# Where the last tile's second layer is cut: column 320 in place of column 256

## The chip, the cores and the metric

The kernel runs on one core of one Trainium2 chip. The metric is the time of one execution in device microseconds; for the kernel before it is the median of three runs.

## The reference

Attention over a sliding window with a few fixed positions at the start, then a layer norm and a two-layer network with a residual. `q`, `k`, `v` are float32 of 4 batches, 8 heads, 768 positions, 64 numbers each.

```python
keep = (key position < 4) | (0 <= query position - key position < 128)
a    = softmax(q @ k.T / sqrt(64), over the keys that are kept)
x    = heads of (a @ v) side by side                   # 4 x 768 x 512
xn   = (x - mean(x)) / sqrt(var(x) + 1e-6) * g_ln
out  = x + relu(xn @ w_ch1) @ w_ch2                    # w_ch1 512 x 2048, w_ch2 2048 x 512
```

The output is float32, 4 x 768 x 512.

## The kernel before

The 3072 rows are 24 tiles of 128 rows; two tiles make a chunk, so there are 12 chunks. Attention runs per tile, the network per chunk.

**How the order is made.** Nothing is issued as it is written down. Each step is an operation with a list of engines that may do it, a planned duration on each, a priority and the buffers that it reads and writes. A planner (`Plan.run`) places the operations by planned time, picks engine and buffer, and then every engine's instructions are emitted in that order. The planned durations are numbers in the program: a matmul group of the second layer counts 0.865 us for 512 columns and in proportion for fewer (line 1078), and the eviction's duration also grows with its width (line 1082).

**The network of a chunk** (`mlp`, from line 1028). The first layer makes eight buffers `h` of 128 x 512 bf16 from the normalised rows, 64 matmuls of 256 columns in all but the first chunk (line 1046), each followed by a relu on ScalarE or VectorE (lines 1056 and 1058). The second layer goes tile by tile. For each tile 16 matmuls, one for each block of 128 of the 2048 hidden values, are summed up in one PSUM bank (line 1074). The weight that is loaded is a 128 x 128 block of `h`, the data that is streamed past it are columns of `w2`. An operation holds four such matmuls.

**The last tile.** For tiles 0 to 22 the second layer is one piece of 512 columns. The last tile, number 23, is divided into pieces by columns: `LAST_CUTS` (line 228) gives the cuts, and the loop of line 1067 runs over the pieces. Each piece has a PSUM buffer of its own, 16 matmuls of its own width, one eviction on VectorE (line 1083: PSUM times the row's factor plus `x`, into `ot` in float32) and one store to `out` (line 1087). So every block of `h` is loaded as a weight once for each piece. The first piece's store is issued by ScalarE's queue, because `len(cuts) - f` is 3 there, which is in `LAST_ACT`; the second piece's is issued by SP.

**What stands at the end.** A check of the softmax sums has been made by then: VectorE counts bad values (line 1114), a small matmul sums them up (line 1119), and a flag is written (line 1121). Every engine reads the flag (line 1159) and branches on it (line 1161); the rare path behind the branch is a slow general kernel that isn't taken here. A tiny matmul (line 1125, "hold") reads the last column of the last tile's `ot` and so makes TensorE wait for the last eviction. SP's last store is kept back until all the rest has been emitted, behind SP's own read of the flag (line 1160), and after its branch SP waits for all outstanding semaphores (in the profile at line 1196).

Of the kernel before, what the change touches and what calls it, by code (L numbers as in the profile page):

```python
# [224 lines left out]
SW_Q = (0.25, 0.7, 0.9)  # L225

LOW, HIGH = 1e-9, 1e9
LAST_CUTS, LAST_ACT = (0, 256, 512), (3,)
NEG = -1e30
NEVER = -1e9  # L230
BIG = 3.3e38
# [969 lines left out]
```

## Time and profile before

| | |
|---|---|
| median of three runs | 216.78 us (216.47, 216.78, 216.9) |
| the profiled execution | 217.02 us |
| its span, first to last instruction | 215.5 us |
| granted TensorE clock over the span | 1.000 |
| TensorE busy | 205.9 us, 96% |
| VectorE, ScalarE, GpSimd busy | 115.3, 110.0, 111.8 us |
| matmuls of the second layer (line 1074) | 84.5 us busy |
| matmuls of the first layer (line 1046) | 79.3 us busy |

PE is TensorE's matmul row and PEld its weight loads, which run beside it. DVE is VectorE, ACT ScalarE, POOL GpSimd, SP SyncE; a q behind a name (SPq) is that engine's queue, with its DMA issues and waits. A line such as `L1074 PE MATMUL one<-w,h` names the line of the kernel, the engine, the instruction, and what is written from what, without buffer numbers. A single matmul's duration in a row is longer than the step from one to the next, because matmuls overlap; what counts in a stream is the step. Some records of matmuls can be missing from a trace.

### The profile page before, as it was taken

What the parts mean: (1) busy time and instruction counts of PE and PEld (TensorE: products, weight loads), DVE (VectorE), ACT (ScalarE), POOL (GpSimd) and SP (SyncE); (2) the same over time, 40 slices, a digit from 0 to 9 for tenths busy, and PEclk for the clock granted to TensorE, in tenths of its full rate; (3) what the DMA queues carried; (4) which work ended last, traced back from release to release, by engine and by line L of the source; (5) the groups of instructions that cost most, each with busy time, mean ns of one, the idle gap of its engine ahead of it and who ended that gap; (6) DMA issues with size and microseconds to landing.
All of it is one profiled execution on the core that took longest, in us unless ns stands there. A gap on an engine that the chain in (4) does not pass through costs nothing.

```text
span 215.5 us, 6660 instructions
## 1 busy us (share of the span) xinstructions
PE 205.9 (96%) x2743; PEld 144.1 (67%) x2765; DVE 115.3 (53%) x315; ACT 110.0 (51%) x178; POOL 111.8 (52%) x166
## 2 busy tenths in 40 slices
PE   7798899999999999999999999999999999999994
PEld 2467875765865875864865865864865865865853
DVE  5589875698445446446345446446355345444011
ACT  3796387496562562562562562562562562530610
POOL 7978632499972881871971981871971211201000
PEclk9999999999999999999999999999999999999999
DMA  5999999999999999799799899899799302202103
GB/s 156 187 190 205 193 206 192 167 180 132 154 187 169 123 125 145 87 175 151 123 115 170 112 147 145 111 122 168 111 141 149 80 3 76 73 0 76 49 2 105
DMA packets 104554, 28.04 MB, mean 130 GB/s; under 512 B 94788, under 2 KB 101576, under 8 KB 104520
## 3 DMA queue, kind: packets, MB, share of 16 engines
q0 software_dynamic: 69872, 13.18, 90.2%
q1 hardware_dynamic: 33448, 13.74, 35.7%
q10 hardware_dynamic: 1200, 0.66, 1.1%
q8 instruction: 22, 0.36, 0.7%
q14 instruction: 12, 0.10, 0.2%
HBM read 27.43 MB, written 6.29 MB: 156 GB/s over the span
## 4 chain that ended last, share of the span: by engine, by line
PE 88%; DVE 5%; DMA 3%; issue 2%; ACT 1%; ACTq 0%; DVEq 0%
PE one L1074 39%; PE one L1046 36%; PE pair L980 3%; DMA natf<-in_q_dram 3%; PE one L953 2%; PE one L960 2%; PE one L969 1%; DVE st L881 1%; DVE xnt L909 1%; PE one L988 1%; PE one L1039 1%; DVE x L873 1%; DVE xc L885 1%; PE pair L605 1%; PE pair L730 1%
## 5 line engine op out<-in xcount | busy, mean ns | idle before, releaser
L1074 PE MATMUL one<-w,h 128*128 128x512 bf16 (+1 forms) x378 | 84.5, 371 | 2.2 <-issue 1.6
L1056 ACT ACTIVATE h<-one 128x512 bf16<-128x512 f32 x93 | 55.6, 598 | 47.3 <-PE one L1046 42.6
L1046 PE MATMUL one<-xnt,w 128*128 128x256 bf16 x704 | 79.3, 273 | 0.0
L1046 PEld LDWEIGHTS <-w 128*128 128x128 bf16 x704 | 68.6, 98 | 10.4
L1074 PEld LDWEIGHTS <-h 128*128 128x128 bf16 x400 | 37.3, 98 | 39.6
L998 ACT ACTIVATE pe<-pair 128x768 bf16<-128x768 f32 x36 | 27.2, 809 | 41.0 <-PE pair L980 41.0
L645 POOL DMA_DIRECT2D vn<-in_v_dram x59 | 38.7, 695 | 10.9 <-DMA w<-in_moe_w_ch_dram 6.8
L890 POOL TENSOR_SCALAR st<-st 128x1 f32<-128x1 f32 x24 | 8.9, 369 | 62.4 <-DVE st L883 61.9
L1021 DVE RECIPROCAL rec<-one 128x4 f32<-128x4 f32 x36 | 6.4, 178 | 62.5 <-PE one L969 51.1
L1083 DVE SCALAR_TENSOR_TENSOR ot<-one,st,x 128x512 f32<-128x512 f32 (+1 forms) x25 | 18.2, 727 | 13.9 <-PE one L1074 9.0
L891 POOL TENSOR_TENSOR st<-st,mhalf 128x1 f32<-128x1 f32 x24 | 17.0, 707 | 2.0
L881 DVE BATCH_NORM_STATS2 st<-x 128x6 f32<-128x512 bf16 x24 | 16.7, 695 | 0.8
L1023 DVE TENSOR_TENSOR x<-one,rec 128x256 bf16<-128x256 f32 x36 | 15.3, 425 | 1.2
L703 POOL DMA_DIRECT2D nat<-in_k_dram x16 | 14.9, 932 | 1.9 <-DMA natp<-in_q_dram 1.6
L703 POOL DMA_DIRECT2D nat<-in_q_dram x16 | 14.3, 905 | 0.0
L1003 DVE TENSOR_TENSOR pe<-pe,band 128x768 bf16<-128x768 bf16 x24 | 12.2, 552 | 0.0
L885 DVE TENSOR_SCALAR xc<-x,st 128x512 bf16<-128x512 bf16 x24 | 9.3, 387 | 0.9
L980 PE MATMUL pair<-qT,kT 64*64 64x128 bf16 (+1 forms) x528 | 9.2, 204 | 0.0
L953 PEld LDWEIGHTS <-pe 128*128 128x128 bf16 (+1 forms) x144 | 6.2, 97 | 2.9 <-issue 0.8
L778 ACT ACTIVATE pe<-pair 128x1024 bf16<-128x1024 f32 (+1 forms) x8 | 7.1, 916 | 1.8 <-PE pair L730 1.4
L1039 PE MATMUL one<-xnt,w 128*128 128x128 bf16 x128 | 8.0, 220 | 0.0
L980 PEld LDWEIGHTS <-kT 64*64 64x64 bf16 x528 | 7.2, 108 | 0.4 <-ACT w L1110 0.4
(112 smaller groups left out, 165.7 us busy)
## 6 DMA issues: line engine op xcount, KB each, us to landing
out_dram<-ot SPq DMA_DIRECT2D x23, 256.0 KB
w<-in_moe_w_ch_dram POOLq DMA_DIRECT2D x8, 512.0 KB, 14.5
nat<-in_k_dram POOLq DMA_DIRECT2D x16, 128.0 KB, 5.1
nat<-in_q_dram POOLq DMA_DIRECT2D x16, 128.0 KB, 5.6
vn<-in_v_dram POOLq DMA_DIRECT2D x44, 32.0 KB, 6.0
vn<-in_v_dram POOLq DMA_DIRECT2D x15, 64.0 KB, 6.3
natp<-in_k_dram POOLq DMA_DIRECT2D x3, 256.0 KB, 14.3
vn<-in_v_dram POOLq DMA_DIRECT2D x6, 128.0 KB, 9.2
```

Source lines behind the costliest of these rows:

```text
L645: P.op(f"vld{t}_{i}", {"POOL": (0.8, 0.85)}, prio + 0.001 * i, lambda e, p0=p0, n=n, hs=hs, src=src: G.dma_start(m.t[p0:p0 + n, hs, 0:64], ...
L703: lambda e, nat=nat, ap=ap: G.dma_start(nat.t, ap), writes=[nat], dma=SW, after=gate(c))
L881: P.op(f"bn{t}", {"DVE": fix(0.60)}, d + 0.12, lambda e: V.bn_stats(st.t[:, 8:14], x.t), reads=[x], writes=[st, mv])
L891: G.tensor_tensor(st.t[:, 16:17], st.t[:, 17:18], mhalf, op=ALU.pow)),
L980: nc.tensor.matmul(pps[u].t[64 * g:64 * g + 64, h2, col + c0:col + c0 + n], lhsT=kt.t[rs, hp, k0:k0 + 64], rhs=qT.t[rs, hp, q0:q0 + n], st ...
L998: nc.scalar.activation(pes[j].t.rearrange("p a b -> p (a b)")[:, 0:768].rearrange("p (a b) -> p a b", a=2), pps[j].t[:, :, 0:384], AF.Exp, ...
L1003: V.tensor_mul(at_s, at_s, band[j] if r > 1 else edge[r][j].unsqueeze(1).to_broadcast([128, 4, 192]))
L1023: P.op(f"x{t - 1}{u}", {"DVE": dve(256)}, d + 0.051 + 0.002 * u, lambda e, u=u, rc=rc, pv=pv: V.tensor_tensor(x.t[:, 256 * u:256 * u + 256 ...
L1046: nc.tensor.matmul(ph.t[:, 256 * s:256 * s + 256], lhsT=w1[ht // 4][:, j, 128 * (ht % 4):128 * (ht % 4 + 1)], rhs=xnt.t[:, j, :], start=j ...
L1056: nc.scalar.activation(hb.t, ph.t, AF.Relu)
L1074: nc.tensor.matmul(pc.t[:, 0:wd], lhsT=(h1[2 * s + i].t[:, 128 * ii:128 * ii + 128] if by_tile else h1[ht // 2].t[:, 256 * (ht % 2) + 128 ...
L1083: V.scalar_tensor_tensor(ot.t[:, sl], in0=pc.t[:, 0:wd], scalar=st.t[:, 16:17], in1=x.t[:, sl], op0=ALU.mult, op1=ALU.add),
```

## The change

The last tile's first piece takes columns 0 to 319 and its second piece columns 320 to 511, 192 of them, where both had 256. The number of matmuls, weight loads, evictions and stores is as before, and so is the engine of each store. The planned durations of the two pieces change with the widths. No other tile is touched.

```diff
-LAST_CUTS, LAST_ACT = (0, 256, 512), (3,)
+LAST_CUTS, LAST_ACT = (0, 320, 512), (3,)
```

## The prediction

> **What bounds the kernel now.** I read the views in this order: the chain of waits over the whole span, to see which engine sets the end; then the chain, the timeline and the groups from 208 us on, which is where the last tile's second layer runs; then the rows on the last stores, because a change at the very end can only act through what comes behind the last matmul.
>
> The chain of the whole span (its share by engine, and three pieces of its 256, each with start, length and number of instructions):
>
> ```profile
> PE 88%; DVE 5%; DMA 3%; issue 2%; ACT 1%; ACTq 0%; DVEq 0%
> ...
> 25.89 1.79 PE one L1039 x32
> ...
> 39.32 1.73 PE one L1074 x8
> ...
> 54.25 6.99 PE one L1046 x64
> ```
>
> TensorE carries 88% of the chain, so the kernel is one long row of matmuls, and a matmul saved anywhere would be worth its own time. The three pieces give what one matmul costs in a row: 1.79 us / 32 = 55.9 ns at 128 columns, 6.99 / 64 = 109.2 ns at 256, 1.73 / 8 = 216.3 ns at 512. From 128 to 256 that is 53.3 ns for 128 columns, from 256 to 512 107.1 ns for 256: 0.417 ns a column both times, with some 2.5 ns on top for each matmul. All three use a new 128x128 weight for every matmul, as the last tile does.
>
> The end of the chain, from 208.6 us on:
>
> ```profile
> 208.55 3.72 PE one L1074 x33
> 212.28 0.03 issue
> 212.31 0.02 DVEq L1083
> 212.33 0.04 issue
> 212.37 0.50 DVE ot L1083
> 212.87 0.04 issue
> 212.91 0.19 PE one L1125 x2
> ```
>
> The reader sees the last 32 matmuls (16 for columns 0 to 255, 16 for 256 to 511; the 33rd is the last of the tile before), then the last eviction on VectorE, then the small matmul that is tied to it. The chain as printed stops there; the store that follows the same eviction is found in the timeline (start, length, instruction, and in brackets the idle time before it):
>
> ```profile
> 208.86 0.75 DVE L1083 SCALAR_TENSOR_TENSOR ot<-one,st,x 128x512 f32<-128x512 f32 x1 [2.61 <-PE one L1074]
> 209.64 3.58 SPq L1087 DMA_DIRECT2D out_dram<-ot  x2
> 210.72 0.48 DVE L1083 SCALAR_TENSOR_TENSOR ot<-one,st,x 128x256 f32<-128x256 f32 x1 [1.11 <-PE one L1074]
> 211.24 0.38 ACTq L1087 DMA_DIRECT2D out_dram<-ot  x1
> 212.37 0.48 DVE L1083 SCALAR_TENSOR_TENSOR ot<-one,st,x 128x256 f32<-128x256 f32 x1 [1.16 <-PE one L1074]
> ```
>
> The row of SP merges the issue for the tile before and the last issue, and ends at 209.64 + 3.58 = 213.22. One such issue takes 0.33 us (row below), so the last store is issued from 212.88 on, 0.03 us after the eviction ended at 212.85. What is moved, by stretch (length; TensorE, weight loads, VectorE, ScalarE, GpSimd; granted clock, share of the 16 DMA engines, GB/s):
>
> ```profile
> L1087 SPq DMA_DIRECT2D out_dram<-ot x2: 332/334/337, 209.6 to 212.9; - x2
> ...
> 210.40:211.35 0.95, 0.95 (x12) 0.85 (x10) 0.48 (x1) 0.00 (x0) 0.00 (x0) 1.00 0.73 276
> 212.10:212.65 0.55, 0.16 (x2) 0.00 (x0) 0.28 (x1) 0.00 (x0) 0.00 (x0) 1.00 0.70 238
> 212.65:213.60 0.95, 0.19 (x2) 0.09 (x2) 0.20 (x1) 0.00 (x0) 0.00 (x0) 1.00 0.02 9
> 213.60:214.10 0.50, 0.00 (x0) 0.00 (x0) 0.00 (x0) 0.00 (x0) 0.00 (x0) 1.00 0.70 244
> 214.10:214.25 0.15, 0.00 (x0) 0.00 (x0) 0.00 (x0) 0.00 (x0) 0.00 (x0) 1.00 0.50 116
> ```
>
> Three bursts stand apart: the store of the tile before (512 columns) from 210.4, the first piece's from 212.1, the second piece's from 213.6. Each begins about 0.8 us after its issue began (209.64, 211.24, 212.88). Behind the last one SP walks through its closing waits, shown here for the stretches 213.7 to 214.48 and 214.5 to 214.7 (shortest, median and longest in ns, first and last start):
>
> ```profile
> L1196 SPq EVENT_SEMAPHORE  x11: 28/28/28, 213.8 to 214.4; - x11
> ...
> L1196 SPq EVENT_SEMAPHORE  x1: 28/28/28, 214.6 to 214.6; - x1
> ```
>
> Eleven waits start between 213.8 and 214.4, one every 0.06 us, and the twelfth at 214.6, about 0.1 us later than that step would have it. By its place it is the one that the last store's landing holds up. The span ends at 215.5, some 0.9 us of closing work later, and the profiled execution took 217.02 us, 1.5 us more than its span.
>
> **The change, part by part.** Before 208.6 us nothing differs: the same instructions in the same order. The planner places work by time, but in the timeline all that starts after the first matmul of this tile is what is quoted above, so no other work is there to be put elsewhere.
>
> *Matmuls.* Sixteen of 256 columns become sixteen of 320, and sixteen of 256 become sixteen of 192. By 0.417 ns a column, 64 columns are 26.7 ns: 135.9 and 82.5 ns. The first piece ends 16 x 26.7 = 0.43 us later, the second takes 0.43 us less, and the last matmul ends where it did: 16 x (135.9 + 82.5) = 3.49 us against 32 x 109.2 = 3.49. No row has 192 or 320 columns; 192 lies between 128 and 256 and 320 between 256 and 512, and these rows stand on one line, so I take zero. The bounds: a straight line cannot make it better than zero, and the loads (first rival) make it at most 0.43 us worse.
>
> *The first piece's eviction and store.* The groups by shape (number, busy us, mean ns, idle us):
>
> ```profile
> L1083 DVE SCALAR_TENSOR_TENSOR ot<-one,st,x 128x512 f32<-128x512 f32 x23 | 17.2, 748 | 11.7 <-PE one L1074 6.8 <-POOL st L891 4.7
> L1083 DVE SCALAR_TENSOR_TENSOR ot<-one,st,x 128x256 f32<-128x256 f32 x2 | 1.0, 484 | 2.3 <-PE one L1074 2.3
> ```
>
> (748 - 484) / 256 = 1.03 ns a column, so 320 columns take 550 ns and 192 take 418. The first eviction starts 0.43 us later, at 211.15, and ends at 211.70. Behind it on VectorE stands the last eviction, which waited 1.16 us for TensorE before and starts at 212.37; 0.67 us of that cover is left. The store on ScalarE's queue is issued at 211.73 and not at 211.24, and nobody but the closing walk waits for that queue. Its transfer starts at 212.6. A 512-column store keeps the engines 0.73 x 0.95 = 0.694 us, a 256-column one 0.70 x 0.55 = 0.385, so 64 columns are (0.694 - 0.385) / 4 = 0.077 us, and it ends near 213.2. The last store's transfer begins at 213.5, so 0.3 us of the gap that was 212.65 to 213.60 stays open. Cost nothing. If that cover were gone, the two would share the same 16 engines and the end would move by what overlaps, 0.46 us at the worst.
>
> *The last eviction.* It starts at the same time and takes 418 ns and not 484: 0.066 us off the path. SP's last issue and the tied matmul both wait for it and move with it, and so does the walk of waits.
>
> *The last store.* It moves three quarters of the bytes in the same 128 row pieces: 0.077 us off, by the same rows. The lead-in of 0.8 us didn't follow the size (512 and 256 columns above), so I leave it. The bounds: nothing, if SP's walk is what ends last, and 0.077 in full, as the twelfth wait is late by about 0.1 us. I take it in full, since 0.1 is more than 0.077, though only just.
>
> The sum: 0 - 0.066 - 0.077 = -0.143 us. On the profiled execution 217.02 becomes 216.88. That execution was 0.24 above the median of the three runs, 216.78, so the prediction is **216.64 us**, 0.07% less. A difference under about 0.2% (0.43 us, as far as the three runs lie apart) is no more than a measurement of this kernel can tell from no change.
>
> **The rivals.**
>
> *Slower: the weight loads set the pace of the narrow piece.* Every matmul needs a fresh load, and these are the loads of this tile and those of the 128-column matmuls:
>
> ```profile
> L1074 PEld LDWEIGHTS <-h 128*128 128x128 bf16 x31 | 3.0, 98 | 0.5
> L1039 PEld LDWEIGHTS <-w 128*128 128x128 bf16 x128 | 7.2, 98 | 0.1
> ```
>
> A load shows 98 ns, and in this tile the loads fill 3.0 of 3.49 us, with little room. At 192 columns a matmul streams 82.5 ns, less than the load; the point at which it would decide is 98 ns, some 230 columns. If the pace could not fall under 98 ns, the second piece would lose 16 x (98 - 82.5) = 0.25 us; if it stayed at today's 109.2, 0.43. With the 0.143 gained, the time would be 0.10 to 0.28 above the median, up to **217.06**. The Trainium skill (TensorE: Matmul & The Clock Gate, "LDWEIGHTS (loading the stationary operand)") has the load time as columns over 1.2, which for 128 is 107 ns, and by that as the pace the piece would lose an estimated 16 x (107 - 82.5) = 0.39 us; it speaks against the change. Against the rival stands the second row: 128 loads of 98 ns fill only 7.2 us, 56 ns apiece, and the first fence has 32 of those matmuls at 55.9 ns. So loads overlap one another, and a pace well under 82.5 ns was kept with the same weight shape. Chance 0.06.
>
> *Slower: the two last stores collide.* The gap of 0.3 us is eaten if the first store's transfer is late by more than that; the worst is 0.46 - 0.14 = 0.32 above the median, **217.10**. The steady lead-in of 0.8 us speaks against it. Chance 0.02.
>
> *Little gained: SP's walk or the closing work ends last.* Then only the eviction's 0.066, or nothing, comes off: **216.71 to 216.78**. For it speaks that the twelfth wait is late by hardly more than the 0.077 I take off. Chance 0.10.
>
> *Faster by more: the store shrinks as a whole.* From issue (212.88) to the twelfth wait (214.6) are 1.7 us; a quarter of that is 0.43, and with the eviction **216.28**, 0.23% less. Against it: the lead-in was alike for 512 and 256 columns, and the walk's own step allows only about 0.1 beyond the eviction. Chance 0.04.
>
> *The cut does something else,* since the planner also uses the widths for its times and could order or place the end differently. With one eviction and one store per piece and nothing else left to run, there is nothing to exchange: **216.78**. Chance 0.02.
>
> **How the numbers follow.** The forecast has 0.76. The runs of before lie 0.31 below to 0.12 above their median; about 216.64 that gives 216.33 to 216.76. Downward the fourth rival's 216.28 is taken in as 216.30. Upward the little-gained case with the same spread reaches 216.90, and the loads' 217.06 nearly closes it: I take **216.30 to 217.05**. Faster by over 0.2% is the fourth rival's 0.04 and 0.05 of the forecast, whose centre lies a third of the way there: 0.09. Slower by over 0.2% needs a slower rival's worst price and an unlucky run: 0.06. The rest, 0.85, is within 0.2%.
>
> **What would show it.** Right: the chain after has the last eviction start near 212.4 as before, 418 ns long, an eviction of 320 columns of 550 ns before it, the first piece's matmuls 136 ns apart and the second's 82 to 83, and the last burst of data a fifth shorter. Wrong: a second piece whose matmuls stand 98 ns or more apart and whose loads leave no idle time (the loads); a first burst that runs into the last (the stores); a twelfth wait that follows the eleventh by 0.06 us (the walk). A median under 216.3 or over 217.1 would mean that something before 208.6 us moved, which no row here explains.

## The result and the profile after

The changed kernel takes 217.38 us, the median of 22 runs (216.93 to 219.02); the kernel before took 216.66 in as many runs of the same comparison. The ratio is 1.0037, with a 95% interval of 1.0027 to 1.0047. So it is 0.7 us slower, where 0.14 us less was forecast, and the time lies above the stated range. Two of the 22 runs, 218.87 and 219.02 us, show a mean granted clock of 0.992 where the others have 0.995 to 1.000; without them the median is 217.30 us.

The profiled execution of the changed kernel hides this at first sight:

```profile
span 215.3 us, 6682 instructions
```

That is 0.2 us less than the span before. But the two executions already differ at the first matmul of the last tile (208.03 us against 208.61), ahead of which the kernels are the same. So the end has to be compared from a mark of its own. I use the start of the last eviction, called M from here on. The chain's end after:

```profile
207.98 3.72 PE one L1074 x33
...
211.80 0.43 DVE ot L1083
212.22 0.04 issue
212.27 0.19 PE one L1125 x2
```

The 33 matmuls take 3.72 us, to the hundredth what they took before. M is 211.80 and the span ends at 215.33, 3.54 us later; before it was 212.37 and 215.53, 3.16 us. The loss of 0.37 us in this execution therefore lies wholly behind the last matmul. The groups and the timeline after:

```profile
L1074 PE MATMUL one<-w,h 128*128 128x320 bf16 x16 | 2.3, 299 | 0.0
L1074 PE MATMUL one<-w,h 128*128 128x192 bf16 x16 | 1.5, 246 | 0.0
...
210.57 0.55 DVE L1083 SCALAR_TENSOR_TENSOR ot<-one,st,x 128x320 f32<-128x320 f32 x1 [1.53 <-PE one L1074]
211.80 0.42 DVE L1083 SCALAR_TENSOR_TENSOR ot<-one,st,x 128x192 f32<-128x192 f32 x1 [0.67 <-PE one L1074]
...
209.07 3.51 SPq L1087 DMA_DIRECT2D out_dram<-ot  x2
211.16 0.38 ACTq L1087 DMA_DIRECT2D out_dram<-ot  x1
```

The evictions last what was forecast (0.55 and 0.42 us) and SP issues the last store 0.45 us behind M, where it was 0.51. What is left is the store itself. In stretches of the trace after (the columns as before: length, busy time of five engines, clock, DMA share, GB/s):

```profile
213.04:213.52 0.48, 0.00 (x0) 0.00 (x0) 0.00 (x0) 0.00 (x0) 0.00 (x0) 1.00 0.66 209
213.52:213.69 0.17, 0.00 (x0) 0.00 (x0) 0.00 (x0) 0.00 (x0) 0.00 (x0) 1.00 0.00 0
213.69:213.99 0.30, 0.00 (x0) 0.00 (x0) 0.00 (x0) 0.00 (x0) 0.00 (x0) 1.00 0.17 48
```

The last burst is in two parts, with a gap in which nothing starts. The DMA queues say what they are, first for 213.04 to 213.52, then for 213.69 to 213.99 (queue, packets, MB, share of 16 engines):

```profile
q1 hardware_dynamic: 135, 0.09, 59.0%
q14 instruction: 1, 0.01, 6.6%
...
q14 instruction: 1, 0.01, 10.7%
q1 hardware_dynamic: 9, 0.01, 6.2%
```

A store is 128 rows and 16 closing packets of 4 bytes, nine packets for each of 16 engines. The first part holds 135 of the 144, that is fifteen engines' share, and the second the nine that are missing. With the first part comes one packet of the instruction queue, 8 KB and by the queue's name a fetch of the program's code: by its record it runs from 213.20 to 213.71, and the first of the eight late rows starts at 213.71. The records don't name the DMA engine of a packet; that the fetch and the late rows share one is read from these times and counts. Fifteen engines have reported their share by 213.86, the sixteenth at 214.38. SP's walk waits for the sixteenth:

```profile
L1196 SPq EVENT_SEMAPHORE  x11: 28/28/28, 213.2 to 213.8; - x11
...
L1196 SPq EVENT_SEMAPHORE  x1: 28/28/28, 214.4 to 214.4; - x1
```

The twelfth wait is now 0.6 us behind the eleventh. The same two views of the kernel before, 213.20 to 213.65 and 213.65 to 214.2:

```profile
q14 instruction: 1, 0.01, 4.6%
...
q1 hardware_dynamic: 142, 0.13, 69.1%
```

The same fetch was there before, from 213.29 to 213.62, and the store's rows started at 213.71. It was over in time by a tenth of a microsecond. What it goes with is ScalarE's branch, before and then after:

```profile
L1161 ACTq COMPARE_BRANCH  x1: 68/68/68, 212.2 to 212.2; - x1
...
L1161 ACTq COMPARE_BRANCH  x1: 68/68/68, 212.1 to 212.1; - x1
```

By the records the branch starts at 212.20 and 212.12 and the fetch 1.09 and 1.08 us later. On ScalarE's queue the read of the flag and the branch stand behind the first piece's store. That store waits for the first piece, which now ends 0.43 us later. So the fetch was carried from just ahead of the last store's rows into their midst. (VectorE's branch is followed by a fetch as well, 1.18 us later in both; it came behind the rows before, and after the delay it meets only the late ones.)

### The profile page after: what moved, and what is told of

The parts are those of the page before. It is cut to its first block, busy times and chain, and to the rows that moved or that the text cites. A ratio compares the mean times of both kernels' runs of the same rounds, so it can differ in the third digit from the quotient of the medians.

```text
span 215.3 us, 6682 instructions
## 1 busy us (share of the span) xinstructions
PE 208.1 (97%) x2765; PEld 143.9 (67%) x2765; DVE 114.7 (53%) x315; ACT 110.0 (51%) x178; POOL 111.3 (52%) x166
## 4 chain that ended last, share of the span: by engine, by line
PE 89%; DVE 5%; DMA 3%; ACT 1%; issue 1%; ACTq 0%; DVEq 0%
PE one L1074 40%; PE one L1046 36%; PE pair L980 3%; DMA natf<-in_q_dram 3%; PE one L953 2%; PE one L960 2%; PE one L969 1%; DVE st L881 1%; DVE xnt L909 1%; PE one L988 1%; PE one L1039 1%; DVE x L873 1%; PE pair L605 1%; PE pair L730 1%; DVE pe L781 1%
## 5 line engine op out<-in xcount | busy, mean ns | idle before, releaser
L1074 PE MATMUL one<-w,h 128*128 128x512 bf16 (+2 forms) x400 | 87.4, 371 | 0.0
L1083 DVE SCALAR_TENSOR_TENSOR ot<-one,st,x 128x512 f32<-128x512 f32 (+2 forms) x25 | 18.2, 726 | 13.9 <-PE one L1074 8.9
L885 DVE TENSOR_SCALAR xc<-x,st 128x512 bf16<-128x512 bf16 x24 | 8.8, 366 | 0.9
```

Source lines behind the costliest of these rows:

```text
L1074: nc.tensor.matmul(pc.t[:, 0:wd], lhsT=(h1[2 * s + i].t[:, 128 * ii:128 * ii + 128] if by_tile else h1[ht // 2].t[:, 256 * (ht % 2) + 128 ...
L1083: V.scalar_tensor_tensor(ot.t[:, sl], in0=pc.t[:, 0:wd], scalar=st.t[:, 16:17], in1=x.t[:, sl], op0=ALU.mult, op1=ALU.add),
```

## The experiments

Theory A, formed from this comparison, is that the fetch behind ScalarE's branch holds one DMA engine while the last store's rows are due there. The rivals are B (narrow row pieces land late of themselves), C (the narrow matmuls), D (a loss that grows smoothly with the cut) and E (the fetches belong to the end of the program, not to the branches). In the table all times are us behind the mark M, from the records of one execution each; "ScalarE" is the start of its branch, "fetch" the start and length of the first 8 KB fetch behind M, "15th" and "16th" the moments at which the last two engines report the last store.

| kernel | ScalarE | fetch | first row | 15th | 16th | span's end | median us |
|---|---|---|---|---|---|---|---|
| before, 256 | -0.17 | 0.92 + 0.33 | 1.34 | 2.18 | 2.21 | 3.16 | 216.66 |
| after, 320 | 0.32 | 1.41 + 0.51 | 1.28 | 2.06 | 2.58 | 3.54 | 217.38 |
| c320_again | 0.32 | 1.46 + 0.58 | 1.27 | 2.06 | 2.74 | 3.70 | 217.46 |
| c320_look | 0.32 | 1.80 + 0.35 | 1.28 | 2.07 | 3.17 | 4.14 | one run |
| c320_act1 | 0.83 | 1.91 + 0.56 | 1.28 | 2.06 | 2.06 | 3.02 | 216.45 |
| c256_split | 0.32 | 1.40 + 0.72 | 1.34 | 2.21 | 2.89 | 4.27 | 217.49 |
| c256_act1 | 0.33 | 1.40 + 0.61 | 1.34 | 2.21 | 2.74 | 3.71 | 217.19 |
| c256_act2 | 0.79 | 1.83 + 0.63 | 1.35 | 2.18 | 2.21 | 3.18 | 216.54 |
| c288 | 0.07 | 1.15 + 0.55 | 1.31 | 2.16 | 2.46 | 3.43 | 216.88 |
| c352 | 0.57 | 1.81 + 0.38 | 1.24 | 2.00 | 2.01 | 2.98 | 216.33 |
| c384 | 0.82 | 1.84 + 0.56 | 1.27 | 2.01 | 2.04 | 3.00 | 216.46 |
| c320_noif | none | none | 1.28 | 2.04 | 2.06 | 2.98 | 216.30 |
| c256_noif | none | none | 1.34 | 2.18 | 2.21 | 3.13 | 216.48 |

In after, c320_again, c320_look, c256_split and c256_act1 the late rows begin when the first fetch ends, within 0.01 us each time. Where VectorE branches ahead of ScalarE, as in c256_act2 and c384, the first fetch stands 1.17 and 1.18 us behind VectorE's branch and is taken for VectorE's.

**c320_again** is the changed kernel with nothing edited.

> The changed kernel once more, as the base of the others on this chip. In its first profile fifteen of the sixteen DMA engines have landed their share of the last store at 213.86 us, the sixteenth only at 214.38. Theory A (a code fetch is in the way): an 8 KB instruction fetch, which follows ScalarE's branch by 1.08 us (212.12 to 213.20; 212.20 to 213.29 before), lies on one DMA engine just as the last store's data comes, and that engine's eight rows wait for it. Theory B (the store itself): the narrower row pieces, 768 B in place of 1024 B, land late of themselves. Theory C (matmuls): the 192-column matmuls are paced by their loads. A and B expect about 217.4 us again, 0.3 to 0.4% over the kernel before; in the trace A expects one engine's eight rows after the fetch, B a late landing without a fetch on it; C expects 98 ns or more between the narrow matmuls.

217.46 us, ratio 1.0042 (1.0026 to 1.0058). The fetch is there, the sixteenth engine is 0.68 us behind the fifteenth, and the narrow matmuls stand 82 to 83 ns apart. That ends theory C.

**c320_act1** has a second read of the flag on ScalarE.

```diff
+        for _ in range(1):
+            nc.values_load(flag, engines=[mybir.EngineType.Activation], min_val=0)
         bad = nc.values_load(flag, min_val=0, max_val=128 * NT * H)
```

> The changed kernel; ScalarE reads the flag one time more before its branch, so that its branch and the fetch behind it come some 0.6 us later (fetch at about 213.8), when the last store's data (213.04 to 213.51) has passed. No width, store or matmul is touched. Theory A: the delay is gone although an instruction was added: 0.14 us under the kernel before, about 216.5 (ratio 0.999). Theories B and C: unchanged at 217.4 (ratio 1.0035).

216.45 us against 216.62, ratio 0.9996 (0.9987 to 1.0005): an instruction more, and the whole loss is gone, though the interval can't tell the kernel from the one before. The queues in 213.05 to 213.52 and in 213.52 to 214.10:

```profile
q1 hardware_dynamic: 144, 0.10, 62.6%
...
q14 instruction: 3, 0.02, 16.5%
q8 instruction: 1, 0.02, 15.5%
```

All 144 packets of the last store lie in the first stretch and all fetches in the second. The matmuls, evictions and the store are the changed kernel's, so B falls. From M to the span's end are 3.02 us, 0.15 less than before. SP's waits here:

```profile
L1198 SPq EVENT_SEMAPHORE  x11: 27/28/28, 213.2 to 213.8; - x11
...
L1198 SPq EVENT_SEMAPHORE  x1: 28/28/28, 213.9 to 213.9; - x1
```

The twelfth wait stands 0.07 us behind the eleventh, hardly more than the walk's own step of 0.06. So the store's gain is only just not hidden by the walk, as the forecast had it.

**c256_split** does the reverse to the kernel before: ScalarE issues the first piece's store in two halves.

```diff
-                     lambda e, sl=sl, ot=ot, b=b, r=r: (nc.sync if e == "SP" else nc.scalar).dma_start(
-                         out[b, 128 * r:128 * (r + 1), sl], ot.t[:, sl]),
+                     lambda e, sl=sl, ot=ot, b=b, r=r: nc.sync.dma_start(
+                         out[b, 128 * r:128 * (r + 1), sl], ot.t[:, sl]) if e == "SP" else [nc.scalar.dma_start(
+                         out[b, 128 * r:128 * (r + 1), h], ot.t[:, h]) for h in (slice(0, 128), slice(128, 256))],
```

> The kernel before (256 and 256 columns); ScalarE issues the first piece's store as two of 128 columns, one issue (0.38 us) more ahead of its branch. Its fetch moves from 213.29 to about 213.7, onto the last store's data (213.68 to 214.23); the last store, the matmuls and the evictions stay as they are. Theory A: slower by 0.4 to 0.8 us, 217.0 to 217.4 (ratio 1.002 to 1.0035), with one engine's rows behind the fetch. Theories B and C: no difference, 216.66, because the last store and the matmuls have their old sizes.

217.49 us, ratio 1.0042 (1.0029 to 1.0055): the changed kernel's loss, with the old cut. Its queues in 213.2 to 213.7 and in 213.97 to 214.35:

```profile
q1 hardware_dynamic: 133, 0.12, 71.5%
q14 instruction: 1, 0.01, 9.0%
...
q8 instruction: 1, 0.02, 20.6%
q1 hardware_dynamic: 9, 0.01, 6.2%
q14 instruction: 1, 0.01, 5.0%
```

Again one engine's nine packets come behind the fetch (two more of other engines' closing packets lie between the stretches). Its span ends later behind M than that of any other, 4.27 us, because the additional store moves the last one to another semaphore: SP meets it as its fifth wait and has the others still to walk.

**c384** moves the cut on.

```diff
-LAST_CUTS, LAST_ACT = (0, 320, 512), (3,)
+LAST_CUTS, LAST_ACT = (0, 384, 512), (3,)
```

> The cut at 384: pieces of 384 and 128 columns. The first store and so ScalarE's branch move a further 0.5 us back, and the fetch comes at about 214.2, behind the last store's data (about 213.5 to 213.8). Theory A: faster than before by two steps of the prediction's sum, 2 x (0.066 + 0.077) = 0.29 us, 216.4 (ratio 0.9987). Theory B: row pieces of 512 B land later still, 217.4 or more. Theory C: 128-column matmuls run at 56 ns in the first chunk, so C gives no loss here, but a loss at 320 alone would be hard to explain by it.

216.46 us, ratio 0.9993 (0.9984 to 1.0001). The loss is gone, as A expected and B did not, but the gain behind M is 0.17 us and not 0.29. The first store now runs into the last: its rows lie up to 1.42 us behind M, and the last store's begin at 1.27. That is the prediction's second rival, met at a later cut; that the overlap costs the missing 0.12 us is likely, but no run tests it by itself.

**c288 and c352** test whether it is the distance of the cut or the meeting with the fetch. The edit is the same line, with 288 and 352.

> The cut at 288: pieces of 288 and 224 columns. The first store and ScalarE's branch move 0.21 + 0.03 us back from the cut at 256, so the fetch comes at about 213.53 where it came at 213.29, and the last store's data begins at about 213.65. Theory A (the fetch holds one engine): a fetch of 0.33 us reaches 0.2 us into the data, one of 0.5 us reaches 0.4; with the 0.07 that the narrower piece gains, 216.75 to 217.0. Theory D (no fetch; the loss grows smoothly with the distance of the cut from 256): 216.62 + 0.4 x 0.8 = about 216.9 here, and then more at 352 than at 320.

> The cut at 352: pieces of 352 and 160 columns. ScalarE's branch moves 0.64 + 0.10 us back, the fetch to about 214.03, and the last store's data lies at 213.57 to 213.95, so the fetch comes just behind it. The first store's data ends near 213.35 and doesn't touch the last. Theory A: the prediction's sum for 96 columns, 0.10 + 0.115 = 0.21 us under the kernel before, 216.41 (ratio 0.999). Theory D: 217.5 or more.

288 takes 216.88 us against 216.72, ratio 1.0003 (0.9995 to 1.0012); the median lies where A expected it, the ratio can't tell it from no change. In its trace the fetch reaches 0.4 us into the rows and the sixteenth engine is 0.30 us late. (Its profiled execution, 217.74 us, is the slowest of its twelve and late already at the last tile's first matmul, 209.05 us; why, the record doesn't show. Only what lies behind M is used of it.) 352 takes 216.33 us, ratio 0.9982 (0.9974 to 0.9991): faster than both kernels. The loss doesn't grow with the cut, it comes and goes, and D falls. Behind M its trace gains 0.18 us, where A expected 0.21; the medians lie 0.39 us apart, and where the rest of that comes from is not shown. The end of c352's timeline:

```profile
210.88 0.58 DVE L1083 SCALAR_TENSOR_TENSOR ot<-one,st,x 128x352 f32<-128x352 f32 x1 [1.75 <-PE one L1074]
211.50 0.38 ACTq L1087 DMA_DIRECT2D out_dram<-ot  x1
211.89 0.38 DVE L1083 SCALAR_TENSOR_TENSOR ot<-one,st,x 128x160 f32<-128x160 f32 x1 [0.42 <-PE one L1074]
212.30 0.33 SPq L1087 DMA_DIRECT2D out_dram<-ot  x1
```

ScalarE's store is issued only 0.8 us ahead of the last one, so that its branch and fetch fall behind the last store's rows, while the first store's rows still end ahead of them.

**c320_noif and c256_noif** leave out the rare path, the reads of the flag and the branches. (The two lines behind the `...` build the slow general kernel.)

```diff
-        bad = nc.values_load(flag, min_val=0, max_val=128 * NT * H)
         order_last.emit(order_last.eng)
-    with tc.If(bad > 0, label="fits"):
-        ...
```

> The cut at 320, with the rare path left out: no flag is read, nothing branches, and the kernel ends behind the last store. Theory A: without the branches there is no 8 KB fetch on the last store's data, all sixteen engines land within 0.2 us, and the kernel is faster than its own twin with the cut at 256 by the prediction's 0.14 us. How much both gain by the missing branches A doesn't say. Theory E (the fetch belongs to the end of the program and not to the branch): the fetches are still there, the sixteenth engine lands late, and it stays 0.5 to 0.8 us above its twin.

> The twin: the cut at 256 with the rare path left out in the same way. Theory A: 0.14 us above the run with the cut at 320. Theory E: 0.5 to 0.8 us under it.

216.30 us (ratio 0.9980, 0.9959 to 1.0002) and 216.48 us (0.9987, 0.9973 to 1.0000). In c320_noif from 208 us to the end of the span the only queues are the stores':

```profile
q1 hardware_dynamic: 288, 0.36, 15.0%
q10 hardware_dynamic: 144, 0.16, 6.9%
```

Without the branches these fetches are gone, which ends theory E. Over the whole span the pages count 12 packets of `q14 instruction` and 22 of `q8 instruction` with the branches, 8 and 21 without: five fewer, and five engines branch. The twins differ by 0.18 us in their medians and by 0.15 behind M. The intervals of the two overlap, so the times alone would not settle such a small step; together with the trace, where each term is found again, they agree with the prediction's 0.14.

**c256_act1 and c256_act2** put the reads of the flag that cured 320 into the kernel before, one and two of them (the edit of c320_act1, with `range(1)` and `range(2)`).

> The kernel before (cut at 256); ScalarE reads the flag one time more before its branch, the edit that took the loss away at 320. At 320 one such read moved ScalarE's branch by 0.53 us, so here the fetch moves from 213.29 to about 213.8, into the last store's data (213.68 to 214.23). Theory A: slower by 0.3 to 0.9 us, 217.0 to 217.6. A rival, that a further read on ScalarE is itself good or harmless wherever it stands: 216.65 or a little under.

> The same with two further reads: the fetch moves by 1.06 us to about 214.35, behind the last store's data. Theory A: the loss of the kernel with one read is gone again, 216.65 as before, although ScalarE does more and branches later. A rival, that it is a late ScalarE that costs time: slower than with one read.

One read: 217.19 us, ratio 1.0037 (1.0019 to 1.0055), with one engine 0.53 us late. Its queues in 214.60 to 215.17 and in 215.34 to 215.70 (as in c256_split, two closing packets lie between):

```profile
q1 hardware_dynamic: 133, 0.12, 62.7%
q14 instruction: 1, 0.01, 6.7%
...
q14 instruction: 1, 0.01, 6.7%
q1 hardware_dynamic: 9, 0.01, 6.5%
```

Two reads: 216.54, ratio 1.0005 (0.9989 to 1.0020), all engines in time. The same instruction harms at one place and is harmless at a later one, so neither the work on ScalarE nor its lateness costs the time. What goes with the loss is the moment of its fetch.

**c320_look** is the changed kernel once more, for the size of the loss.

> The changed kernel for one more profile. The stretch from the last tile's first matmul to the end of the span was 7.30 and 7.46 us in its two profiles against 6.78 with the fetch moved away, a loss of 0.52 and 0.68 us, while the medians differ by 0.9. If theory A is all, the loss of a run varies with how the fetch meets the rows, and a slower run shows a stretch of 7.5 to 8.2 us with one engine's rows still later; if something ahead of the last tile adds to the loss, the stretch stays near 7.4 and the first matmul of the last tile comes later than 208.4.

One run, 217.66 us. Its last tile starts at 208.17 us (208.03 and 208.35 in the kernel's other two profiles), and from there to the span's end are 7.90 us, 1.12 more than in c320_act1. The queues in 213.20 to 213.65, 213.65 to 214.06 and 214.06 to 214.45:

```profile
q1 hardware_dynamic: 135, 0.09, 62.8%
...
q14 instruction: 2, 0.02, 13.8%
...
q8 instruction: 1, 0.02, 17.9%
q1 hardware_dynamic: 8, 0.01, 6.5%
q14 instruction: 1, 0.01, 5.5%
```

Fifteen engines' packets lie in the first stretch; the sixteenth's eight rows come in the third, behind one fetch and with others beside them. So one execution loses 0.5 us and another 1.1, and the medians' difference (217.4 against 216.45) lies between. Here the first fetch on record starts 1.47 us after ScalarE's branch and not 1.08; what held that engine until then is not on record, and stays open. So does why the same fetch lasts 0.51 us in one execution and 0.58 in another.

## Why the prediction was wrong

**Held, term by term.** *Matmuls:* forecast 136 ns and 82 to 83 ns apart with no change in the sum; the 33 matmuls took 3.72 us both times. The loads as pace (the first rival) did not occur: loads of 98 ns each overlapped, and the steps were 82.5 ns. By the Trainium skill (TensorE: Matmul & The Clock Gate, "LDWEIGHTS (loading the stationary operand)") a load takes its columns over 1.2, an estimated 107 ns for 128; that is not the pace here either. *Evictions:* 550 and 418 ns forecast, 550 and 416 measured. *The last store:* 0.077 us off was forecast; with the fetch out of the way (c320_act1) the sixteenth engine reports 2.06 us behind M and not 2.21, which is 0.15 less, 0.07 of it the eviction's and 0.08 the transfer's. *The sum:* in c320_act1 the stretch behind M is 0.15 us shorter than before, and without branches (the twins) 0.15 too; forecast 0.143.

**Failed: the step "The first piece's eviction and store", priced at nothing.** It followed the moved store on ScalarE's queue as far as its rows and stopped there: "nobody but the closing walk waits for that queue". The flag's read, the branch and the fetch that follow the store on the same queue moved with it by 0.49 us against M, into the last store's rows. Their price is 0.52 us (after), 0.68 (c320_again) and 1.12 (c320_look) from the first matmul of the last tile to the span's end, each against c320_act1, and 0.93 us by the medians (217.38 against 216.45). The notice was there to be had: the page lists `q14 instruction`, and the stretch ahead of the last burst held one 8 KB packet that had only a tenth of a microsecond to spare. The prediction sought transfers that collide only among the stores.

**The rivals.** "The two last stores collide" named the right kind of event at the wrong partner; at 320 the first store's rows end well ahead of the last store's. "Little gained" and "faster by more" did not occur: with the fetch out of the way the gain was the sum's. Nor did "the cut does something else" by another order of the work: TensorE's weight loads, VectorE's and ScalarE's instructions stand in the same order in both kernels' traces.

**The range.** It reached to 217.05 by a rival that cost at most 0.43 us. Nothing in it stood for work behind a moved instruction on its own queue.

The Trainium skill (DMA: Bandwidth & Descriptors, "Queues, rings and completion order") has each DMA engine serve its queues in turn, and lists a queue row for refills of the runtime's own; and ("Why a DMA increments its semaphore by 16 and not by 1") a store as done only when all engines that carry it have reported. The traces agree with both: after the change eight rows of the store begin at 213.71, when the fetch ends, and fifteen engines in time and one 0.5 us late hold up the whole store.

## What to carry to other kernels

When an instruction is moved, follow its queue to the end, past the last useful instruction: here a branch and the code fetch behind it were moved by half a microsecond and landed on the last store. At the end of a kernel look at the DMA queues by packets, instruction fetches included, and see how much room each neighbour of the last store has; a tuned end may stand a tenth of a microsecond from a cliff. And when two profiles are compared, set a mark near the change: here the slower kernel's profile had the shorter span.

## What the runs showed of the hardware

The branch past the rare path was followed by an 8 KB fetch of code. Behind ScalarE's branch it started 1.08 to 1.09 us later in five traces (before, after, c256_split, c256_act1, c288), 1.14 in c320_again and 1.47 in c320_look; behind VectorE's 1.18 us later in both kernels. At the kernel's end such a fetch took 0.31 to 0.72 us, and eight rows of a store, one DMA engine's share, came after it.

The granted clock can be lower for some microseconds near the start of an execution. In the profiled one of c384 it was 0.57 and 0.86 from 9 to 15 us, where the kernel before has 1.00 in both rows:

```profile
9.00:12.00 3.00, 2.58 (x37) 1.95 (x37) 1.05 (x3) 2.38 (x4) 2.27 (x3) 0.57 1.76 185
12.00:15.00 3.00, 3.00 (x52) 1.73 (x54) 2.85 (x7) 1.87 (x3) 2.10 (x3) 0.86 1.83 179
```

That execution took 217.93 us where the median is 216.46, and it reached the last tile at 209.57 us; its stretch behind M is among the shortest. The profiled execution of c256_act1 shows 0.57 in the first of these rows as well. For both the table compares only what lies behind M.
